# Dense pooled values: block-diagonal zeros taken out of an attention and gated-MLP kernel, and its order drawn up anew

## The chip, the cores and the metric

The kernel runs on one core of a Trainium2 chip. The metric is the device time of one execution in microseconds (us). TensorE is called PE, its weight loads PEld, VectorE DVE, ScalarE ACT, GpSimd POOL, and SyncE, which issues the DMAs here, SP.

## The reference

```python
B, H, S, D = 8, 8, 576, 64; factor = 4; Sd = S // factor; scale = 1 / sqrt(D)
q_d, k_d, v_d = (a.reshape(B, H, Sd, factor, D).mean(axis=3) for a in (q, k, v))
out_d = softmax(scale * q_d @ k_d.T) @ v_d            # pooled: 144 x 144
mask = abs(pos[:, None] - pos[None, :]) < factor      # local: 7 keys for a query
out_local = softmax(where(mask, scale * q @ k.T, -1e9)) @ v
attn = repeat(out_d, factor, axis=2) + out_local
x = attn.transpose(0, 2, 1, 3).reshape(B * S, H * D)  # 4608 x 512
out = (sigmoid(x @ w_gate) * (x @ w_val)) @ w_out     # 512 -> 1536 -> 512
```

All of it in fp32; q, k and w_gate are drawn some 6, 6 and 3 times larger than usual.

## The kernel before

**Units.** The attention is cut into 32 units, each two heads of one batch (unit u = 4 x batch + pair), with the two heads on the two halves of the 128 partitions. Units 0 to 7 (batches 0 and 1) are written in `early`, the other 24 in `later`. A unit's steps, by the names used below: loads `qk` (local q and k), `qkd` and `vd` (the same data with the four elements of a pool group side by side) and `vb` (v for the local part); `pb` sums q and k over the four, `vB` sums v; `s` makes the local scores, `sd` the pooled ones; both softmaxes go over DVE, ACT and POOL; `tt` and `dt` turn the weights; `od` is the pooled output and `x` the local one; `xa` adds them and `xh`, `xl` split the sum into two fp16 parts for the MLP.

**Block-diagonal operands.** `od` and the local `x` need a different v for each head. Before, v of the two heads stands in a 128x128 block-diagonal tile (`vdblk`, and `vtile` in `vflat`): the first head's 64 columns on the first 64 partitions, the second's on the others, zeros elsewhere, so that one product of 128x128 serves both. The zeros are set once at the start, and whoever fills a tile writes its two halves apart: `load_vb` with two DMAs, `vdb` and `vB` with two additions. `sd` and `s` multiply the heads apart, on 64 rows each.

**MLP.** 4608 tokens in nine chunks of 512. Weights come as 64-bit words, are put together by `pr` (ACT), `sh` and `jn` (DVE) and split into two fp16 parts (`hi` on ACT, `lo` on DVE). Chunk 0 makes 12 gate products `pg`, 12 value products `pv` and the output products `po`; it needs x of units 0 to 3 for its first `pg`. Chunk 1 does the same. Later chunks multiply pairs of blocks in seven products instead of eight (`bank`, `obank`), from sums of x that DVE and POOL prepare.

**The order.** All steps are entered as operations with an engine, a cost in us, what they follow, and the buffers they hold. A list scheduler in the kernel then places them, engine by engine, by due times (`GOALS`, `PACE`); its table of costs and goals sets the order in which each engine's instructions are written. Each engine runs its own instructions in that order and waits for the others by semaphores. Where the schedule leaves PE idle before the first `pg`, dummy products `awake` are put in.

Of the kernel before, what the change touches and what calls it, by code (L numbers as in the profile page):

```python
# [10 lines left out]
F32 = mybir.dt.float32  # L11
# [11 lines left out]
PACE = {'a0': -6.52, 'a': 6.04, 's0': 25.62, 'sp': 8.122, 'e': 2.9, 's': 0.15, 'sd': 0.65, 'tt': 13.18, 'dt': 13.95, 'do': 15.81, 'x': 16.17, 'b3': -0.21, 'b4': -2.69, 'b5': -3.01, 'b6': -1.13, 'b7': 3.85, 'extra': 0.41, 'ahead': 36}  # L23
GOALS = {'x0': 40.8, 'x0s': 7.26, 'pv': 72.16, 'pvs': 6.2, 'x1': 101.2, 'x1s': 19.48, 'po': 221.56, 'pos': 26.01, 'c1': 151.79}
INTURN = ("s", "sd", "tt0_", "tt1_", "dn", "dt", "vB", "do", "x0", "x1")
# [35 lines left out]
VTOF = (0, 1, 2, 3, 0, 1, 2, 0)  # L61
# [14 lines left out]
def attention_moe(ctx, tc, qk, qkd, v, vd, wg, wv, wo, mask, out):  # L76
# [68 lines left out]
    def zeroed(eng, shape, dtype, name):  # L145
# [4 lines left out]
    vdblk = [zeroed(nc.gpsimd, [P, NKC, P], F32, f"vdblk{i}") for i in range(2)]  # L150
    ad = zeroed(nc.gpsimd, [QM, 2, NKC, 2, WIN], F32, "ad")
    vblk = cp.tile([P, 2, NBLK, P], F16, tag="vblk", name="vblk")
    vring = cp.tile([P, NVR, NBLK * D], F32, tag="vring", name="vring")
    vflat = [x.rearrange("p (a b) -> p a b", a=NBLK) for x in (
        vring.rearrange("p a b -> p (a b)")[:, : NBLK * P], vring.rearrange("p a b -> p (a b)")[:, NBLK * P : 2 * NBLK * P],
        vblk.rearrange("p t b c -> p (t b c)").bitcast(F32), borrow(0, NBLK * P))]
    for i, t in enumerate(vflat):
        (nc.gpsimd if i % 2 else nc.vector).memset(t, 0.0)
    flat = {id(vblk): vblk.rearrange("p t b c -> p (t b c)").bitcast(F32)}
# [160 lines left out]
    def vload(u):  # L320
        vraw[u] = vring[:, NVR - 1 if u < NPLAIN else u % NVR].rearrange("p (a b) -> p a b", a=NBLK)
        nc.sync.dma_start(vraw[u], v[u])
# [124 lines left out]
    def zero(*tiles):  # L447

        for t in tiles:
            nc.gpsimd.memset(flat[id(t)], 0.0)  # L450
            own(t, "zero")
# [1351 lines left out]
```

## Time and profile before

| | |
|---|---|
| median of 3 runs | 989.0 us (986.9 to 991.27) |
| the profiled execution | 988.05 us, span 986.3 us |
| PE busy | 952.4 us, 97% of the span |
| DVE busy | 805.4 us, 82% |
| ACT busy | 656.9 us, 67% |
| POOL busy | 419.5 us, 43% |

The span reaches from the first to the last instruction. The busy time of PE holds its dummy products too, and the end of a matmul in the trace is modelled, so what a run of matmuls costs is read from its start to the start of the next operation.

### The profile page before, as it was taken

What the parts mean: (1) busy time and instruction counts of PE and PEld (TensorE: products, weight loads), DVE (VectorE), ACT (ScalarE), POOL (GpSimd) and SP (SyncE); (2) the same over time, 40 slices, a digit from 0 to 9 for tenths busy, and PEclk for the clock granted to TensorE, in tenths of its full rate; (3) what the DMA queues carried; (4) which work ended last, traced back from release to release, by engine and by line L of the source; (5) the groups of instructions that cost most, each with busy time, mean ns of one, the idle gap of its engine ahead of it and who ended that gap; (6) DMA issues with size and microseconds to landing.
All of it is one profiled execution on the core that took longest, in us unless ns stands there. A gap on an engine that the chain in (4) does not pass through costs nothing.

```text
span 986.3 us, 23787 instructions
## 1 busy us (share of the span) xinstructions
PE 952.4 (97%) x9412; PEld 738.1 (75%) x9412; DVE 805.4 (82%) x1430; ACT 656.9 (67%) x1650; POOL 419.5 (43%) x411
## 2 busy tenths in 40 slices
PE   7788999999999999989999999999999999999997
PEld 5654655455547677778888888888888988888885
DVE  6999998879999889889998888878788678556653
ACT  5888665656446776768777787777776865655551
POOL 4331323555456666445666565565543323000000
PEclk8999999999999999999999999999999999999999
DMA  9898888444435788677867766777555656666631
GB/s 313 287 316 274 295 300 262 161 169 153 178 137 197 255 278 251 191 264 273 285 237 259 269 234 249 231 283 269 200 203 193 231 179 217 214 220 209 230 128 44
DMA packets 78736, 225.36 MB, mean 228 GB/s; under 512 B 26656, under 2 KB 30240, under 8 KB 78368
## 3 DMA queue, kind: packets, MB, share of 16 engines
q1 hardware_dynamic: 78624, 223.83, 66.0%
q8 instruction: 74, 1.21, 0.5%
q14 instruction: 38, 0.31, 0.1%
HBM read 196.80 MB, written 27.00 MB: 227 GB/s over the span
## 4 chain that ended last, share of the span: by engine, by line
PE 78%; DVE 7%; issue 1%; ACT 1%; DVEq 0%
PE bank L868 35%; PE obank L1007 15%; PE po L431 10%; PE pg L431 4%; PE pv L431 4%; PE x L431 2%; PE s L436 2%; PE sd L436 2%; PE od L431 2%; PE at L555 1%; DVE wg L751 1%; DVE vblk L607 1%; PE adt L575 1%; DVE arena L748 1%; DVE wo L965 1%
## 5 line engine op out<-in xcount | busy, mean ns | idle before, releaser
L868 PE MATMUL bank<-arena,wv 128*128 128x256 f16 x1764 | 220.8, 273 | 5.4 <-DVE wg L898 4.0
L868 PE MATMUL bank<-arena,wg 128*128 128x256 f16 x1764 | 221.2, 273 | 0.1
L868 PEld LDWEIGHTS <-wv 128*128 128x128 f16 x1764 | 170.8, 98 | 31.5 <-issue 7.4
L868 PEld LDWEIGHTS <-wg 128*128 128x128 f16 x1764 | 171.4, 98 | 24.9 <-issue 1.0
L1007 PE MATMUL obank<-wo,spare 128*128 128x256 f16 x1071 | 147.3, 273 | 0.6 <-DVE wo L965 0.6
L1007 PEld LDWEIGHTS <-spare 128*128 128x128 f16 x1071 | 103.2, 98 | 13.9 <-issue 1.7
L965 DVE SCALAR_TENSOR_TENSOR wo<-wg,wo 128x512 f16<-128x512 f32 (+1 forms) x136 | 93.5, 705 | 19.8 <-ACT wo L962 19.5
L751 POOL TENSOR_TENSOR wg<-wg 128x256 f32<-128x256 f32 x50 | 40.9, 820 | 160.3 <-DVE wo L965 141.8
L962 ACT ACTIVATE wo<-wg 128x512 f16<-128x512 f32 (+1 forms) x136 | 76.4, 577 | 16.1 <-DVE wg L898 9.2
L431 PE MATMUL po<-spare,wo 128*128 128x512 f16 x324 | 79.4, 379 | 1.2 <-ACT arena L1138 1.2
L910 ACT COPY wv<-bank 128x512 f32<-128x512 f32 x84 | 49.1, 584 | 37.2 <-PE bank L868 36.3
L431 PEld LDWEIGHTS <-wo 128*128 128x128 f16 x432 | 40.8, 98 | 41.3 <-issue 2.8
L917 ACT COPY bank<-wv 128x256 f32<-128x256 f32 x84 | 31.7, 377 | 54.6 <-DVE wg L915 43.7
L431 PE MATMUL pv<-arena,wv 128*128 128x512 f16 x288 | 67.5, 384 | 0.1
L431 PE MATMUL pg<-arena,wg 128*128 128x512 f16 x288 | 67.4, 384 | 0.1
L915 DVE TENSOR_TENSOR wg<-bank,wv 128x512 f32<-128x512 f32 x63 | 43.4, 689 | 27.7 <-PE bank L868 25.9
L1007 PE MATMUL obank<-wo,wv 128*128 128x256 f16 x357 | 58.4, 273 | 0.0
L545 POOL TENSOR_TENSOR ad<-e,sme 72x288 f32<-72x288 f32 x48 | 37.6, 800 | 45.5 <-PE adt L575 27.7
L607 DVE SCALAR_TENSOR_TENSOR vblk<-vring,svb,vblk 64x640 f16<-64x640 f32 x48 | 54.7, 1139 | 0.6
L748 POOL TENSOR_TENSOR arena<-arena 128x512 f16<-128x512 f32 (+1 forms) x33 | 37.1, 1128 | 42.5 <-ACT arena L744 41.0
L517 POOL TENSOR_TENSOR t<-t,sm 128x768 f32<-128x768 f32 x24 | 38.1, 1586 | 33.5 <-DVE sm L523 22.7
L431 PEld LDWEIGHTS <-wg 128*128 128x128 f16 x288 | 27.8, 99 | 32.6 <-issue 2.3
(215 smaller groups left out, 2004.2 us busy)
## 6 DMA issues: line engine op xcount, KB each, us to landing
wg<-wg SPq DMA_DIRECT2D x42, 896.0 KB, 4.7
wv<-wv SPq DMA_DIRECT2D x42, 896.0 KB, 4.6
spare<-wo SPq DMA_DIRECT2D x51, 448.0 KB, 4.6
qk<-in_qk_dram SPq DMA_DIRECT2D x30, 610.0 KB, 4.8
qkd<-in_qkd_dram SPq DMA_DIRECT2D x29, 576.0 KB, 5.3
arena<-in_wo_dram SPq DMA_DIRECT2D x24, 512.0 KB, 5.3
vd<-in_vd_dram SPq DMA_DIRECT2D x29, 384.0 KB, 5.1
out_dram<-arena SPq DMA_DIRECT2D x16, 512.0 KB, 5.1
```

What stands on the lines that cost most here:

```text
L431: nc.tensor.matmul(o, w[a], x[c], start=first and i == 0, stop=last and i == len(pairs) - 1)
L436: nc.tensor.matmul(o, w, x, start=True, stop=True)
L517: engine(n("sb" if k == "mx" else "tm")).tensor_tensor(out=groups(), in0=groups(), in1=s[k].unsqueeze(2).to_broadcast([P, 4 * NH, WIN]), o ...
L607: nc.vector.scalar_tensor_tensor(out=VB[ps, 1, :, ps], in0=src, scalar=sc, in1=VB[ps, 0, :, ps], op0=ALU.mult, op1=ALU.subtract)
L748: eng.tensor_tensor(out=lo, in0=src, in1=hi, op=ALU.subtract)
L751: eng.tensor_tensor(out=o, in0=x, in1=y, op=ALU.subtract)
L868: nc.tensor.matmul(o, w[:, a, k], x[:, xb, k, c], start=start and z == 0, stop=z == len(mms) - 1, skip_group_check=True)
L910: op(f"sa_{n}_{i}", "A", 0.58, lambda i=i: nc.scalar.copy(snap(i)[:, HC:], banks[i]), [g(0), p("ad"), p("se")] + (["w1"] if n == 0 else []))
L915: lambda i=i: nc.vector.tensor_tensor(out=vsum(n) if i else duo(n)[:, 1], in0=banks[i], in1=snap(i)[:, :CH], op=ALU.add),
L962: nc.scalar.activation(g()[:, blocks, 0], src.rearrange("p (b t) -> p b t", t=HC), AF.Copy, scale=GSCALE)
L965: nc.vector.scalar_tensor_tensor(out=g()[:, blocks, 1], in0=src.rearrange("p (b t) -> p b t", t=HC), scalar=GSCALE, in1=g()[:, blocks, 0], ...
L1007: nc.tensor.matmul(obank[M][:, half], w[:, wb, a], g[:, xb, x], start=start and z == 0, stop=z == 5, skip_group_check=True)
```

## The change

It has four parts. First, the pooled v (`vdense`) and the v of the local part in units 0 to 7 are held dense, 64 columns for both heads; the products `od` and `x` are made by `heads`, one for each half: 64 rows by 64 columns, into that half's output partitions. The zeroing of the block-diagonal tiles falls away, `load_vb` is one DMA, `vB` one addition. Second, in batch 0 only q is summed in `pb`; the sum over k is made by PE, which accumulates four products whose moving operand steps over every fourth element, and the sum over v likewise, with the v factor as the stationary operand. Third, v of units 0 to 6 has seven buffers of its own instead of four. Fourth, the costs, goals and pace of the scheduler are new, and the order is made from them.

```diff
-GOALS = {'x0': 40.8, 'x0s': 7.26, 'pv': 72.16, 'pvs': 6.2, 'x1': 101.2, 'x1s': 19.48, 'po': 221.56, 'pos': 26.01, 'c1': 151.79}
+GOALS = {'x0': 50.0, 'x0s': 4.73, 'pv': 87.23, 'pvs': 5.86, 'x1': 94.08, 'x1s': 17.53, 'po': 220.49, 'pos': 30.55, 'c1': 162.23}
...
-VTOF = (0, 1, 2, 3, 0, 1, 2, 0)
+VTOF = (0, 1, 2, 3, 4, 5, 6, 0)
...
-    vdblk = [zeroed(nc.gpsimd, [P, NKC, P], F32, f"vdblk{i}") for i in range(2)]
+    vdense = [cp.tile([P, NKC, D], F32, tag=f"vdense{i}", name=f"vdense{i}") for i in range(2)]
...
-    for i, t in enumerate(vflat):
-        (nc.gpsimd if i % 2 else nc.vector).memset(t, 0.0)
...
     def load_vb(u):
         vtile[u] = vflat[VTOF[u]]
-        for ps in HALVES:
-            nc.sync.dma_start(vtile[u][ps, :, ps], v[u][ps])
+        nc.sync.dma_start(vtile[u], v[u])
...
+    def heads(o, w, x, first=True, last=True):
+
+        pairs = ((0, 0), (0, 1), (1, 0)) if len(w) == 2 else ((0, 0),)
+        for i, (a, c) in enumerate(pairs):
+            for ps in HALVES:
+                nc.tensor.matmul(o[ps], w[a][ps], x[c][ps], start=first and i == 0, stop=last and i == len(pairs) - 1)
...
         def vB():
             own(VDB, u)
-            for ps in HALVES:
-                nc.gpsimd.tensor_tensor(out=VDB[ps, :, ps], in0=y()[ps, :, 0], in1=y()[ps, :, 1], op=ALU.add)
+            nc.gpsimd.tensor_tensor(out=VDB.rearrange("p a b -> p (a b)"), in0=y()[:, :, 0], in1=y()[:, :, 1], op=ALU.add)
...
             for c in range(NKC):
-                product(pt[:, :SD], [VDB[:, c]], [s["adt"][:, c]], c == 0, c == NKC - 1)
+                heads(pt[:, :SD], [VDB[:, c]], [s["adt"][:, c]], c == 0, c == NKC - 1)
...
         def prep():
             x = qkdraw[u].rearrange("p (g f) -> p g f", f=4)
+            if first:
+                s["qd"] = wk.tile([P, 2, SD], F32, tag="qks", name=f"qks_{u}", bufs=1)[:, 0]
+                s["kd"] = [x[:, SD:, f] for f in range(4)]
+                x = x[:, :SD]
+                if chosen[n("pb")] == "V":
+                    nc.vector.tensor_reduce(s["qd"], x, axis=AX.X, op=ALU.add)
+                    return
...
         def pooled():
...
+            if first:
+                for qb in range(2):
+                    for f in range(4):
+                        for h, ps in enumerate(HALVES):
+                            nc.tensor.matmul(pts[h][:QM, qb * SD : (qb + 1) * SD], s["qd"][ps, qb * QM : (qb + 1) * QM], s["kd"][f][ps],
+                                             start=f == 0, stop=f == 3)
+                return
...
         def dout():
...
+            if first:
+                for c in range(NKC):
+                    for f in range(4):
+                        heads(pt[:, :SD], [vdraw[u][:, c, :, f]], [s["adt"][:, c]], c == f == 0, c == NKC - 1 and f == 3)
+                return
...
             for i in range(i0, i1):
-                product(pt[:, (i - i0) * R : (i - i0 + 1) * R], [vtile[u][:, i]], [s["at"][:, i]])
+                heads(pt[:, (i - i0) * R : (i - i0 + 1) * R], [vtile[u][:, i]], [s["at"][:, i]])
```

On SP, at the start of the program, the loads of units 0 to 3 stand like this before (`wo`, `wv` and `wg` are weight buffers that are borrowed for early units; the `in_v_dram` rows are `vb`, the `in_wg_dram` ones the MLP's weights):

```order
L399 DMA wo_116<-in_qkd_dram 128x1152
L407 DMA vd_184<-in_vd_dram 128x768
L407 DMA wv_115<-in_vd_dram 128x768 x3
L391 DMA qk_250<-in_qk_dram 128x1220
L414 DMA vring<-in_v_dram 64x10x64 x2
L399 DMA wo_116<-in_qkd_dram 128x1152
L391 DMA wo_116<-in_qk_dram 128x1220
L414 DMA vring<-in_v_dram 64x10x64 x2
L399 DMA wo_116<-in_qkd_dram 128x1152
L391 DMA wo_116<-in_qk_dram 128x1220
L414 DMA vblk<-in_v_dram 64x10x64 x2
L414 DMA wg_114<-in_v_dram 64x10x64 x2
```

The same stretch of SP with the change, up to the first two weight rows:

```order
L396 DMA wo_116<-in_qkd_dram 128x1152
L388 DMA qk_180<-in_qk_dram 128x1220
L404 DMA vd_233<-in_vd_dram 128x768
L404 DMA wv_115<-in_vd_dram 128x768 x3
L396 DMA wo_116<-in_qkd_dram 128x1152
L388 DMA wo_116<-in_qk_dram 128x1220
L396 DMA wo_116<-in_qkd_dram 128x1152
L410 DMA vring<-in_v_dram 128x640
L388 DMA wo_116<-in_qk_dram 128x1220
L410 DMA vring<-in_v_dram 128x640 x3
L223 DMA arena<-in_wg_dram 128x1024
L223 DMA arena<-in_wv_dram 128x1024 x2
```

Unit 1's q and k (`qk`) now stand ahead of the pooled v, units 2's and 3's pooled q and k ahead of the first v, and each v is one row of 128x640.

On PE, before the first `pg`, unit 2's turn of the pooled weights, of the local ones and its `od` stand like this before:

```order
L1282 MATMUL adt_616<-ident,ad 128x72 x6
L93 LDWEIGHTS idle
L93 MATMUL awake<-idle 128x256
L1237 MATMUL at_0_632<-ident,t_406 128x2x64 x3
L1237 MATMUL at_1_640<-ident,t_406 128x2x64 x3
L431 MATMUL od_654<-adt_2_617,vdblk_117 128x144 x3
```

And with the change, with unit 1's local output `x` among them:

```order
L1295 MATMUL adt_658<-ident,ad 128x72 x6
L448 MATMUL x_0_668<-at_1_515,vring 64x58 x16
L448 MATMUL x_1_688<-at_1_515,vring 64x58 x4
L1243 MATMUL at_0_695<-ident,t_382 128x2x64 x3
L448 MATMUL od_710<-adt_2_659,wv_115 64x144 x24
L1243 MATMUL at_1_744<-ident,t_382 128x2x64 x3
```

`od` has 24 products of half the height where it had three, and reads the raw v in `wv`; the dummies here are gone; `x` has 20 products of 64 rows where it had ten of 128.

On POOL, where the first units of `later` begin, the sums of v stand like this before (`vd` is the loaded v, `qkd` the loaded q and k, `ad` the pooled weights):

```order
L634 TENSOR_TENSOR qkd_1862<-qkd_1862 128x288x2
L1271 TENSOR_TENSOR ad<-e_1823,sme_1824 72x2x3x48 x2
L634 TENSOR_TENSOR vd_1830<-vd_1830 128x192x2
L585 TENSOR_TENSOR vdblk_117<-vd_1830 64x3x64 x2
L768 TENSOR_TENSOR arena<-wg_114 128x1024
L634 TENSOR_TENSOR vd_2051<-vd_2051 128x192x2
L585 TENSOR_TENSOR vdblk_119<-vd_2051 64x3x64 x2
```

With the change:

```order
L630 TENSOR_TENSOR vd_1572<-vd_1572 128x192x2
L630 TENSOR_TENSOR qkd_1693<-qkd_1693 128x288x2
L581 TENSOR_TENSOR vdense_117<-vd_1572 128x192
L1284 TENSOR_TENSOR ad<-e_1576,sme_1577 72x2x3x48 x2
L1492 MEMSET vblk 128x1280
L1359 TENSOR_TENSOR arena<-spare,arena 128x448
L1234 TENSOR_TENSOR t_1174<-t_1174,sm_1675 128x768
L630 TENSOR_TENSOR vd_1881<-vd_1881 128x192x2
L581 TENSOR_TENSOR vdense_118<-vd_1881 128x192
```

The second sum of v is one row of 128x192 where it was two of 64x3x64.

## Rows read from the trace of the kernel before

**Rows 1.** The page: the span, and of each engine the busy time, its share of the span and the instructions.

```profile
span 986.3 us, 23787 instructions
PE 952.4 (97%) x9412; PEld 738.1 (75%) x9412; DVE 805.4 (82%) x1430; ACT 656.9 (67%) x1650; POOL 419.5 (43%) x411
```

**Rows 2.** Busy time by stretch: the stretch, its length, busy time (and instructions) of each engine, the granted clock of PE as a share of full speed, the busy share of the DMA engines, GB/s.

```profile
0.00:55.38 55.38, 44.50 (x592) 36.02 (x592) 45.24 (x93) 39.20 (x121) 21.66 (x33) 0.94 0.91 301
55.38:148.40 93.02, 85.78 (x552) 46.42 (x547) 88.42 (x183) 68.96 (x164) 27.41 (x29) 0.96 0.87 294
148.40:987.00 838.60, 822.13 (x8277) 655.66 (x8275) 671.69 (x1155) 548.78 (x1367) 370.39 (x349) 1.00 0.63 216
...
10.00:30.00 20.00, 15.23 (x198) 12.32 (x198) 13.69 (x32) 14.23 (x48) 9.83 (x14) 0.83 0.97 280
30.00:55.38 25.38, 20.77 (x307) 17.61 (x305) 24.60 (x52) 21.31 (x65) 7.52 (x9) 1.00 0.90 323
...
100.00:125.00 25.00, 24.53 (x190) 14.27 (x189) 24.10 (x47) 15.43 (x40) 9.57 (x9) 1.00 0.88 286
...
300.00:600.00 300.00, 289.70 (x3233) 239.42 (x3232) 264.84 (x449) 219.67 (x584) 177.96 (x167) 0.99 0.74 254
```

**Rows 3.** The same view of the dummy products `awake` alone: stretch, length, PE busy (and instructions), clock, DMA.

```profile
0.00:55.38 55.38, 13.27 (x81) 0.94 0.91 301
```

**Rows 4.** PE's instructions in order of time before the first `pg`: start, length, line, operation, output<-input, shape (rows*columns of the weights, then output), count; in brackets the idle time before and what ended it. An fp32 product counts as two.

```profile
7.22 0.71 PE L436 MATMUL sd<-qks 64*72 64x144 f32 x8
...
18.61 1.56 PE L1212 MATMUL s<-qk 64*64 64x64 f32 x48 [1.99 <-DMA qk<-in_qk_dram]
...
27.60 0.71 PE L436 MATMUL sd<-qks 64*72 64x144 f32 x8
28.24 0.60 PE L1282 MATMUL adt<-ident,ad 72*128 72x72 f32 x6
...
39.35 0.90 PE L431 MATMUL od<-adt,vdblk 128*128 128x144 f32 x6
40.09 0.60 PE L93 MATMUL awake<-idle 128*128 128x256 bf16 x4
...
50.82 2.44 PE L431 MATMUL x<-at,wg 128*128 128x58 f32 x20
53.10 1.36 PE L93 MATMUL awake<-idle 128*128 128x256 bf16 x11
...
54.58 0.87 PE L1212 MATMUL s<-qk 64*64 64x64 f32 x48
55.38 0.82 PE L431 MATMUL pg<-arena,wg 128*128 128x512 f16 x3
```

**Rows 5.** SP's queue in order of time: start and length of the issuing of DMAs.

```profile
13.17 1.36 SPq L391 DMA_DIRECT2D wo<-in_qk_dram x1
14.63 3.89 SPq L414 DMA_DIRECT2D vring<-in_v_dram x2
18.56 0.97 SPq L399 DMA_DIRECT2D wo<-in_qkd_dram x1
19.57 0.43 SPq L391 DMA_DIRECT2D wo<-in_qk_dram x1
20.10 3.92 SPq L414 DMA_DIRECT2D vblk<-in_v_dram x2
24.11 4.05 SPq L414 DMA_DIRECT2D wg<-in_v_dram x2
28.21 1.40 SPq L226 DMA_DIRECT2D arena<-in_wg_dram x1
```

**Rows 6.** The DMA view of 10 to 32 us in 40 slices of 0.55 us: busy share of the DMA engines in tenths, GB/s, and the packets with their sizes.

```profile
DMA  9999999999999999999999999999997311490969
GB/s 385 413 408 391 432 443 412 345 279 278 188 251 250 278 398 414 355 269 271 183 236 298 260 360 401 400 290 238 177 237 178 91 28 37 98 223 18 145 259 432
DMA packets 6534, 6.08 MB, mean 276 GB/s; under 512 B 5384, under 2 KB 5384, under 8 KB 6531
```

**Rows 7.** DVE's first instructions in order of time, columns as in rows 4.

```profile
1.21 1.12 DVE L158 MEMSET vring<- 128x1280 f32 x1 [0.22 <-issue]
2.56 1.12 DVE L158 MEMSET vblk<- 128x1280 f32 x1 [0.22 <-issue]
...
5.82 1.35 DVE L1197 TENSOR_REDUCE qks<-qkd 128x288 f32<-128x1152 f32 x1 [0.69 <-DMA qkd<-in_qkd_dram]
7.09 0.41 DVE L237 TENSOR_SCALAR wg<-wg 128x512 int32<-128x512 int32 x1
7.54 0.69 DVE L241 SCALAR_TENSOR_TENSOR wg<-arena,wg 128x512 int32<-128x512 int32 x1
```

**Rows 8.** The instructions on the tile `vdblk`, by engine: count, least/median/longest ns, first and last start in us, shapes; and POOL's sums of v by line, with their busy time and mean ns.

```profile
L585 POOL TENSOR_TENSOR vdblk<-vd x48: 525/612/1394, 157.6 to 741.0; 64x192 f32<-64x192 f32 x48
...
L1292 DVE TENSOR_REDUCE vdblk<-wv x2: 935/942/949, 30.6 to 31.6; 64x192 f32<-64x768 f32 x2
...
L585 POOL TENSOR_TENSOR vdblk<-vd 64x192 f32<-64x192 f32 x48 | 35.1, 730 | 9.8 <-PE od L431 7.3
```

**Rows 9.** All engines in order of time around 424 us, columns as in rows 4.

```profile
422.42 2.30 POOL L545 TENSOR_TENSOR ad<-e,sme 72x288 f32<-72x288 f32 x1 [2.56 <-PE adt L575]
...
423.78 0.41 DVE L816 TENSOR_TENSOR arena<-spare 128x256 f32<-128x256 f32 x1
...
424.23 2.83 DVE L816 TENSOR_TENSOR arena<-arena,spare 128x256 f32<-128x256 f32 x1
...
429.33 2.11 PE L868 MATMUL bank<-arena,wv 128*128 128x256 f16 x12 [2.34 <-DVE wg L898]
```

More of the change, by code (lines that the diff above doesn't have):

```diff
@@ L1290, in vdb @@
             if chosen[n("vB")] == "V":
-                for ps in HALVES:
-                    nc.vector.tensor_reduce(VDB[ps, :, ps], vdraw[u][ps], axis=AX.X, op=ALU.add)
+                nc.vector.tensor_reduce(VDB, vdraw[u], axis=AX.X, op=ALU.add)
                 return
             nc.gpsimd.tensor_tensor(out=x[:, :, 0:2], in0=x[:, :, 0:2], in1=x[:, :, 2:4], op=ALU.add)
-            for ps in HALVES:
-                nc.gpsimd.tensor_tensor(out=VDB[ps, :, ps], in0=x[ps, :, 0], in1=x[ps, :, 1], op=ALU.add)
+            nc.gpsimd.tensor_tensor(out=VDB.rearrange("p a b -> p (a b)"), in0=x[:, :, 0], in1=x[:, :, 1], op=ALU.add)
         def dout():
@@ L1356, in early @@
         unit_op("vd", "D", 1.3, lambda: load_vd(u), new=[] if ring else [("vd", "vd_")])
-        unit_op("vb", "D", 1.7, lambda: load_vb(u), new=[(f"vt{VTOF[u]}", "v_")])
-        unit_op("pb", "V", 1.27, prep, ["qkd"], new=[("qks", "qks_")], use=["qkd_"], alt=("P", 2.1))
+        unit_op("vb", "D", 1.3, lambda: load_vb(u), new=[(f"vt{VTOF[u]}", "v_")])
+        unit_op("pb", "V", 0.68 if first else 1.27, prep, ["qkd"], new=[("qks", "qks_")], use=["qkd_"], alt=("P", 1.2 if first else 2.1))
         unit_op("s", "E", 1.3, scores, ["qk", "mq!"], new=[("bank", "s0_"), ("bank", "s1_"), ("t", "t_")], use=["qk_"])
@@ L1372, in early @@
                     use=[f"a{par}_", "at_"])
-        unit_op("sd", "E", 0.75, pooled, ["pb"], new=[("bank", "d0_"), ("bank", "d1_"), ("e", "e_")], use=["qks_"])
+        unit_op("sd", "E", 1.7 if first else 0.75, pooled, ["pb"], new=[("bank", "d0_"), ("bank", "d1_"), ("e", "e_")], use=["qks_", "qkd_"] if first else ["qks_"])
         for h in range(2):
             unit_op(f"dm{h}_", "V", 0.44, lambda h=h: dtop(h), ["sd"], use=[f"d{h}_"])
-            unit_op(f"de{h}_", "A", 1.35, lambda h=h: dexp(h), [f"dm{h}_"] + ["de0_"] * h,
+            unit_op(f"de{h}_", "A", 1.2, lambda h=h: dexp(h), [f"dm{h}_"] + ["de0_"] * h,
                     use=[f"d{h}_", "e_"])
@@ L1379, in early @@
         unit_op("rd", "V", 0.16, lambda: recip("sme"), ["sec"])
-        unit_op("dn", "A" if first else "P", 1.62 if first else 1.5, dnorm, ["rd"], new=[("ad", "ad_")], use=["e_"])
+        unit_op("dn", "A" if first else "P", 1.4 if first else 1.5, dnorm, ["rd"], new=[("ad", "ad_")], use=["e_"])
         unit_op("dt", "E", 0.5, dturn, ["dn"], new=[("bank", "ta_"), ("adt", "adt_")], use=["ad_"])
         unit_op("dc", "A", 0.53, dturned, ["dt"], use=["ta_", "adt_"])
-        unit_op("vB", "V", 1.75, vdb, ["vd", "vm"], new=[(f"vdb{u % 2}", "vdb_")], use=["vd_"], alt=("P", 2.35))
-        unit_op("do", "E", 0.8, dout, ["dc", "vB"], new=[("bank", "do_"), ("od", "od_")], use=["adt_", "vdb_"])
+        if first:
+            unit_op("do", "E", 1.7, dout, ["dc", "vd"], new=[("bank", "do_"), ("od", "od_")], use=["adt_", "vd_"])
+        else:
+            unit_op("vB", "V", 0.95, vdb, ["vd", "vm"], new=[(f"vdb{u % 2}", "vdb_")], use=["vd_"], alt=("P", 1.6))
+            unit_op("do", "E", 0.6, dout, ["dc", "vB"], new=[("bank", "do_"), ("od", "od_")], use=["adt_", "vdb_"])
         unit_op("oc", "A", 0.43, dcopy, ["do"] + ["vs0!"] * first, use=["do_", "od_"])
@@ L1472, in attention_moe, with zero @@
     op("arena", "N", 0.0, lambda: None, ["st1", "st3", "pv11"] + [f"loo{i}_" for i in range(NFC)])
-    op("zero", "P", 3.3, lambda: zero(vblk), ["x16"])
+    def zero():
+        nc.gpsimd.memset(vblk32, 0.0)
+        own(vblk, "zero")
+    op("zero", "P", 1.3, zero, ["x15", "x16"])
     op("head", "A", 0.62, lambda: nc.scalar.copy(xf(2)[:, :, : 2 * WIN], head), ["arena"] + [f"xl{u}" for u in range(NPAIR, NPLAIN)])
@@ L1543, in all_turns @@
         return sorted(t, key=lambda k: t[k])
[L1546 removed]
+    CAPS = dict(qk=2, qkd=1, vd=1, vt0=1, vt1=1, vt2=1, vt3=1, vt4=1, vt5=1, vt6=1, qks=1, t=3, at=2, e=1, ad=1, adt=1, vdb0=1, vdb1=1, od=2, xs=1, stage=NST, wa=2,
                 tanh=2, g16=3, att=2, gate=1, val=1, o0=1, o1=1, o2=1, o3=1)
```

64 lines of the change are left out of this document (30 added, 34 removed).

## The prediction

> **What bounds the kernel now.** I read the page first, for the totals: PE is busy 952 of 986 us, DVE 805 [rows 1]. Busy shares hide stages, so next the busy times in three stretches cut at PE's first gate product (55.38 us) and at its first output product (148.40 us) [rows 2]. After 148.40 PE is busy 822.1 of 838.6: there PE is the bound, and the reader sees 10.3 of its 16.5 idle us between 300 and 600. Between the cuts DVE is busy 88.4 of 93.0 and PE 85.8: DVE leads, until PE catches up (24.5 of 25 us busy from 100 on). Before 55.38 nothing is full: DVE has 45.2, and of PE's 44.5 us 13.3 are `awake`, dummy products [rows 3]. So the third place to look is the start. PE's timeline shows the scores of unit 1 waiting 1.99 us for the load of its q and k [rows 4]. SP's own timeline says why the load is late: the two half-loads of a v tile hold the queue for about 3.9 to 4.1 us, three times, and the first weights after the opening one are issued at 28.21 [rows 5]. In the DMA view of 10 to 32 us, 5384 of 6534 packets are under 512 B, the rate falls from 385-443 to below 250 GB/s, and at 27 to 29 us the queues run nearly dry [rows 6]. DVE is idle 6.3 of the 20 us from 10 to 30 and 0.8 of the 25 after that [rows 2]. The start is paced by loads until about 30 us and by DVE from there.
>
> **The change, part by part.**
>
> *v loaded whole.* Eight units' v arrives in one piece of 128x640 instead of two of 64x10x64, and the queue is reordered so that unit 1's q and k go ahead of the pooled v. The DMA view moved 6.08 MB in 22 us at a mean of 276 GB/s; at the 400 GB/s of its own slices with big packets the same bytes take 15.2, so loads at the end of this stretch can be up to 6.8 us earlier [rows 6].
>
> *PE work in batch 0.* The pooled scores `sd` took 0.64 us from their first product to the next operation (27.60 to 28.24) and now have four times the products in equal pairs: 2.56, +1.92. The pooled output `od` took 0.74 (39.35 to 40.09); three products become 24 half-size ones, twelve pairs: 2.96 if a pair costs what one whole product did, +2.22. The local output `x` took 2.28 (50.82 to 53.10); its 10 products become 10 pairs of 64x64 products. The nearest row is that of the scores, whose 48 matmuls of 64x64 run four at a time, 12 rounds in 0.80 us (54.58 to 55.38), 0.067 a round; 20 rounds are 1.33, -0.95. If pairs do not run side by side it is 2.67, +0.39 [rows 4]. Per unit +3.19, four units +12.8, and all of it lies where PE now runs dummies.
>
> *DVE and POOL before the first gate product.* DVE loses two memsets of 1.12, two q/k sums of 1.35 for three of half the size (an estimate: 0.7 each), and one block-diagonal v sum of 2 x 0.94 [rows 7, 8]. That is 2.2 + 0.6 + 1.9; but the memsets end before the first pooled load lands and DVE waits 0.69 for that load [rows 7], so they give nothing: 2.5 counts.
>
> *When the first gate product starts.* Two bounds. PE: real work so far 44.5 - 13.3 = 31.2, plus 12.8 is 44.0; from the first `sd` at 7.22 that ends at 51.2 if PE never waits. DVE: 45.2 - 2.5 - 2.2 of work and 10.1 + 2.2 of idle make 52.9, and if earlier loads halve its 6.3 idle us, 49.7. I take 51.5, 3.9 earlier, between 49.7 and 55.4 (no gain, if the longer `sd` and `od` eat it). DVE does not carry all of that onward: by the order it has by then joined two weight tiles fewer (two shifts and joins, 2 x (0.41 + 0.69) = 2.2) [rows 7], and has more of unit 4's softmax done. I take 1.3 of it as owed, so the lead that the DVE-bound stage starts with is **-2.6** (0 to -4.4).
>
> *x of units 4 to 7.* -0.95 each on PE. Unit 4's falls into the DVE-bound part, the other three where PE is full: **-2.9** (-3.8 to +1.6).
>
> *od of units 4 to 31.* Three whole products become six halves. If pairs run side by side, as row-split `sd` and four-way `s` do [rows 4], **0**; if not, +0.74 x 24 = +17.8 in the PE-bound part alone. I take 0: a quarter-array round of 0.067 us for four is hard to explain with products in single file. What the scores do not show is two products from different row halves going to one PSUM bank, as the new pairs do; their two row halves go to two banks.
> The Trainium skill, "TensorEngine Tiling (Array Packing)", Restrictions and Gotchas, says of exactly this that different row tiles cannot access the same PSUM bank at the same time. By that rule the pairs would go in single file and the sum would be some 25 us worse (the second rival); no row here shows it either way.
>
> *Strided operands in batch 0.* The k and v factors are now read by PE at every fourth element. No row has a strided operand; the lower bound is nothing, the upper is that `sd` and `od` take twice as long, (2.56 + 2.96) x 4 = 22 us more before the first gate product. I take nothing, since a 4-byte PE pass here already moves half a column per cycle (0.120 us for 144 columns at 2.4 GHz, from 0.74 / 6), and keep the upper end as a rival.
> The Trainium skill, "SBUF — State Buffer", Door 1, says that accesses which each cross into a new 16-byte line pay a penalty; a step of four fp32 is exactly one line. By it the strided passes are slower, and with the upper end as their price the run would come to 995.7 (the third rival); no row here shows it.
>
> *v sums of later units.* POOL's two half-size additions per unit (48, mean 730 ns, 35.1 us) become one [rows 8]: some 17.5 us off POOL. POOL has room. But DVE pays beside it: one 128x256 subtraction took 2.83 where its twin just before took 0.41, while POOL ran a 2.30 us operation, and PE then waited 2.34 us for DVE [rows 9]. The order also hands six of DVE's subtractions on x (L751) to POOL. Of the 10.3 idle PE us between 300 and 600 I take off **-1.5** (0 to -6). The whole later order is shuffled as well, which may put DVE's long passes elsewhere: +8 at worst, about today's idle time again.
>
> **Sum.** -2.6 - 2.9 + 0 - 1.5 = -7.0: span 979.3. The profiled execution took 988.05 for a span of 986.3, so 1.75 lies outside: 981.05. Its own time is 0.95 below the median 989.0, so **982.0**.
>
> **Rivals.**
> *The start gains nothing.* The longer `sd` and `od` sit in each unit's chain (+4.1 a unit), and if chains, not loads, set DVE's idle time, the first product stays at 55.4. For it: DVE's idle gaps before 30 us are waits on PE as well as on loads. Against: PE has 13 us of dummies. -2.9 - 1.5 remain at most, or -2.0 with half of them: 984.5 to 988. Chance 0.20.
> *Pairs in single file* (slower than before). Mechanism: both halves of `od` and `x` write one bank and PE runs them one after the other. +17.8 later, 4 x (2.96 + 1.33) = 17.2 more before the first gate product, which then starts at 68.4, 13.0 later, less the 7.2 idle us that PE has in the next stage, and +1.6 for `x` of units 4 to 7: 986.3 + 25.2, as a run 1014. It decides from about 0.3 us per later `od` on, where 24 of them eat the 7.0. Chance 0.07.
> *Strided reads at half speed* (slower). +22 on PE: first gate product at 73, 17.7 later; the next stage has 7.2 idle us to give back and `x` 3.8: +6.7, 995.7. If only `sd` pays, 10.2, the give-back covers it. Chance 0.05.
> *The new order stalls PE elsewhere* by up to 8: 983 to 991. Chance 0.10, half of it slower than 0.5%.
> *More than forecast*: start at 49.7 (-4.4), `x` in full (-3.8), half the later idle gone (-6): 974.8. Chance 0.13.
> *The forecast*, 978 to 986: 0.45, most of it below 984.
>
> **Chances.** 0.5% (4.9 us) is about what a measurement of this kernel can tell from no change. Faster: 0.13 + 0.42 = 0.55. Same: 0.20 + 0.03 + 0.05 = 0.28. Slower: 0.07 + 0.05 + 0.05 = 0.17. The range 973 to 994 leaves out the single-file case, most of the strided one and the far end of the gain.
>
> **What would show it.** Right: unit 1's scores start at about 12 us, not 18.61, and no v load holds SP for 3 us; the first gate product near 51.5 with some 10 dummies' less time; `od` of later units at 0.74 and `x` of 58 f32 columns at about 1.3; DVE full from 30 to 100. Wrong: a later `od` above 1 us (single file), `sd` of batch 0 above 3 us (strided), the first gate product at 55 or later, or PE idle over 18 us after the first output product.

## The result and the profile after

The changed kernel took 1002.8 us (median of four runs, 1002.6 to 1003.7), the kernel before beside it 988.1: 1.013 times as long, with a 95% interval of 1.011 to 1.016 (the two medians alone give 1.015). The forecast was 982.0, its range 973 to 994: the change is slower, and by more than the range allows.

The page of the changed kernel, lines as in [rows 1]:

```profile
span 1000.5 us, 24849 instructions
PE 971.6 (97%) x9971; PEld 739.3 (74%) x9971; DVE 804.0 (80%) x1420; ACT 659.4 (66%) x1650; POOL 397.9 (40%) x375
```

PE, busy for 97% of the span as before, is busy 19.2 us longer, and 24 without the dummies (48 of them now, 8.1 us, where 81 took 13.3 [rows 3]). The same three stretches as in [rows 2], cut at the first gate product and at the first output product of this kernel (columns as there):

```profile
0.00:60.20 60.20, 56.34 (x903) 43.75 (x903) 36.55 (x87) 38.06 (x125) 11.85 (x19) 1.00 0.74 279
60.20:166.52 106.32, 94.15 (x740) 49.18 (x736) 100.04 (x191) 74.55 (x175) 33.73 (x34) 0.90 0.82 285
166.52:1000.00 833.48, 821.14 (x8335) 646.36 (x8333) 667.41 (x1144) 546.77 (x1353) 352.33 (x324) 1.00 0.62 214
```

All that is lost is lost ahead of the first output product: it comes at 166.5 us in place of 148.4, 18.1 later (4.8 in the first stretch, 13.3 in the second). Behind it the new kernel is 3.9 us quicker. The start has changed hands: PE is busy 56.3 of 60.2 us, and DVE, busy 45.2 of 55.4 before, only 36.6 of 60.2. PE's timeline says with what (columns as in [rows 4]):

```profile
12.71 0.89 PE L1218 MATMUL s<-qk 64*64 64x64 f32 x48
...
22.93 3.22 PE L448 MATMUL od<-adt,vd 64*64 64x144 f32 x48
26.08 4.30 PE L1258 MATMUL sd<-wo,qks 64*72 64x144 f32 x32
30.31 0.55 PE L1243 MATMUL at<-ident,t 128*128 128x128 f32 x3
...
42.81 1.38 PE L448 MATMUL x<-at,vring 64*64 64x58 f32 x40
44.12 0.55 PE L1243 MATMUL at<-ident,t 128*128 128x128 f32 x3
```

From start to start, `od` of batch 0 takes 3.15 us, `x` 1.31, and `sd` 4.23, where it was forecast at 2.56. What that does to DVE is in its waits up to 62 us (what waited, for whom, us in all, times, longest):

```profile
DVE mxd L1265 <- PE sd L1258: 7.9, 3, 3.3
DVE qks L1194 <- PE sd L1258: 4.4, 1, 4.4
```

DVE stands still for 12.3 us because a pooled score is not ready or its input not yet free; before, the first of these waits was 0.2 us and the second not there. In the next stretch PE pays: of its 12.2 idle us (7.2 before) most are waits for DVE.

```profile
PE mxt L266 <- DVE hmx L194: 3.9, 1, 3.9
PE mxt L266 <- DVE vm L334: 2.7, 1, 2.7
PE pg L427 <- DVE wg L260: 2.4, 2, 1.9
PE od L448 <- DVE spare L1343: 1.8, 1, 1.8
```

Before, the waits of that stretch were spread over POOL, DVE, a load and ACT:

```profile
PE at L1237 <- POOL t L1228: 2.0, 1, 2.0
PE adt L1282 <- DVE t L1221: 1.7, 1, 1.7
PE s L1212 <- DMA qk<-in_qk_dram: 1.5, 1, 1.5
PE at L1237 <- ACT at L1240: 1.0, 1, 1.0
```

The granted clock of the stretch (the mean, as a share of full speed) is lower too, 0.90 where it was 0.96, so part of the 8.4 us that PE is busy longer there can be clock and not work: in e13 below, the same products at 0.98 keep it busy 6.7 us less. Whether the lower clock adds to the delay or only follows from PE's waits, no run here tells.

### The profile page after: what moved, and what is told of

The parts are those of the page before. It is cut to its first block, busy times and chain, and to the rows that moved or that the text cites. A ratio compares the mean times of both kernels' runs of the same rounds, so it can differ in the third digit from the quotient of the medians.

```text
span 1000.5 us, 24849 instructions
## 1 busy us (share of the span) xinstructions
PE 971.6 (97%) x9971; PEld 739.3 (74%) x9971; DVE 804.0 (80%) x1420; ACT 659.4 (66%) x1650; POOL 397.9 (40%) x375
## 4 chain that ended last, share of the span: by engine, by line
PE 78%; DVE 17%; issue 3%; ACT 1%; DMA 0%; DVEq 0%; SPq 0%; ACTq 0%
PE bank L864 36%; PE obank L1003 16%; PE po L427 6%; PE pv L427 3%; PE od L448 3%; PE pg L427 3%; PE x L427 2%; PE s L432 2%; PE sd L432 1%; PE sd L1258 1%; PE at L552 1%; DVE wo L260 1%; DVE spare L1106 1%; DVE vblk L603 1%; DVE arena L812 1%
## 5 line engine op out<-in xcount | busy, mean ns | idle before, releaser
L864 PEld LDWEIGHTS <-wv 128*128 128x128 f16 x1764 | 170.3, 98 | 28.6 <-issue 4.7
L747 POOL TENSOR_TENSOR wg<-wg 128x256 f32<-128x256 f32 x62 | 50.6, 818 | 175.6 <-DVE wo L961 130.1
L961 DVE SCALAR_TENSOR_TENSOR wo<-wg,wo 128x512 f16<-128x512 f32 (+1 forms) x136 | 95.9, 726 | 19.8 <-ACT wo L958 19.5
L427 PE MATMUL pg<-arena,wg 128*128 128x512 f16 x288 | 70.1, 393 | 2.4 <-DVE wg L260 2.4
L427 PEld LDWEIGHTS <-wo 128*128 128x128 f16 x432 | 40.1, 98 | 43.1 <-issue 2.6
L744 POOL TENSOR_TENSOR arena<-arena 128x512 f16<-128x512 f32 (+1 forms) x33 | 40.0, 1217 | 57.7 <-ACT arena L740 57.7
L427 PEld LDWEIGHTS <-wv 128*128 128x128 f16 x288 | 28.3, 100 | 34.6 <-issue 4.0
```

Of the source, the lines that this page charges most:

```text
L427: nc.tensor.matmul(o, w[a], x[c], start=first and i == 0, stop=last and i == len(pairs) - 1)
L744: eng.tensor_tensor(out=lo, in0=src, in1=hi, op=ALU.subtract)
L747: eng.tensor_tensor(out=o, in0=x, in1=y, op=ALU.subtract)
L864: nc.tensor.matmul(o, w[:, a, k], x[:, xb, k, c], start=start and z == 0, stop=z == len(mms) - 1, skip_group_check=True)
L961: nc.vector.scalar_tensor_tensor(out=g()[:, blocks, 1], in0=src.rearrange("p (b t) -> p b t", t=HC), scalar=GSCALE, in1=g()[:, blocks, 0], ...
```

## The experiments

Two theories. T1: PE's accumulated sums, above all the strided k, make PE the bound of the start, DVE waits there, and what DVE did not get done delays the next stretch. T2: the new order as such puts the weight work late. All runs are in one table. A ratio is to executions of the kernel before that were made beside that run, whose median lies between 988.1 and 990.4; where two rows are compared, the ratios say more than the medians. The last three columns are of the one profiled execution, which lies above the median by 4.7 us in e11, 2.6 in e17, 2.5 in e6 and 1.4 in e9, and below it by 2.2 in e7 and 1.8 in e5. e3, e6 and e8 do not give the reference's result: they show what an order costs in time, and are no versions to use.

| kernel | us, median | ratio to before (95%) | first gate product | first output product | behind it |
|---|---|---|---|---|---|
| before | 988.1 | | 55.4 | 148.4 | 837.9 |
| the change | 1002.8 | 1.0132 (1.0106 to 1.0159) | 60.2 | 166.5 | 834.0 |
| e1 k in blocks | 996.6 | 1.0067 (1.0052 to 1.0083) | 55.8 | 161.0 | 833.8 |
| e17 k every second | 997.0 | 1.0071 (1.0052 to 1.0089) | 57.1 | 163.6 | 833.8 |
| e2 k summed on DVE, POOL | 995.7 | 1.0060 (1.0041 to 1.0079) | 54.8 | 159.5 | 833.9 |
| e5 and v to a quarter | 993.6 | 1.0049 (1.0031 to 1.0068) | 51.9 | 155.6 | 834.1 |
| e4 true costs | 997.5 | 1.0079 (1.0059 to 1.0099) | 64.3 | 164.2 | 831.4 |
| e3 old goals | 1010.2 | 1.0203 (1.0186 to 1.0219) | 59.5 | 167.4 | 841.1 |
| e8 k in blocks, true costs | 1026.4 | 1.0382 (1.0357 to 1.0407) | 59.2 | 160.7 | 864.1 |
| e7 dense only, new plan | 987.9 | 0.9989 (0.9974 to 1.0004) | 55.2 | 152.3 | 831.6 |
| e6 dense only, old plan | 995.2 | 1.0064 (1.0041 to 1.0087) | 52.5 | 150.0 | 845.9 |
| e9 e7, `od` four times | 994.6 | 1.0048 (1.0028 to 1.0068) | 61.6 | 162.9 | 831.3 |
| e10 e9, `sd` six times | 996.9 | 1.0079 (1.0055 to 1.0104) | 63.8 | 163.1 | 831.3 |
| e11 e7, mixed goals | 987.0 | 0.9987 (0.9962 to 1.0012) | 51.1 | 153.8 | 835.7 |
| e12 e11, old costs | 996.0 | 1.0065 (1.0041 to 1.0089) | 51.3 | 159.8 | 835.8 |
| e13 the change, half joins | 997.5 | 1.0071 (1.0050 to 1.0092) | 60.8 | 160.1 | 835.6 |
| e14 before, half joins | 989.3 | 0.9982 (0.9956 to 1.0007) | 54.9 | 150.4 | 838.8 |
| e15 e7, maxima on ACT | 991.0 | 1.0011 (0.9988 to 1.0033) | 53.4 | 149.8 | 837.3 |
| e16 e11, maxima on ACT | 985.7 | 0.9961 (0.9943 to 0.9979) | 54.0 | 145.8 | 838.0 |

### The stride of the moving operand

In e1, e17, e2 and e5 every engine's instructions stand in the order of the change. In e1 the elements that one product reads lie side by side; in e17 they are two apart.

```diff
# e1
-                s["kd"] = [x[:, SD:, f] for f in range(4)]
+                kf = qkdraw[u][:, S:].rearrange("p (f g) -> p f g", f=4)
+                s["kd"] = [kf[:, f] for f in range(4)]
# e17
+                kf = qkdraw[u][:, S:].rearrange("p (a g f) -> p a g f", a=2, f=2)
+                s["kd"] = [kf[:, f // 2, :, f % 2] for f in range(4)]
```

> The changed kernel, in which batch 0's k is laid out in memory in four blocks of 144, so that the moving operand of each pooled score product has its elements side by side; the order on every engine is that of the change, instruction for instruction. Theory T1 (the operand with a stride of four elements is what I priced wrongly, and TensorE binds the start): the 32 instructions of one unit's pooled scores fall from 4.23 us to 2.1 to 2.6 us, the first gate product from 60.2 us to 52.5 to 55, and the time from 1002.8 us by 5 to 8 to 995 to 998. Theory T2 (the new order binds: VectorE's weight joins stand late, so that the weight loads and the stage after wait for them): the pooled scores fall as much, the first gate product comes a few us earlier at most, and the stage behind it gives that back: 1000 to 1003.

> The change with batch 0's k laid out so that the moving operand of the pooled scores takes every second element (in the change every fourth, 4.30 us for the 32 instructions of a unit; side by side 2.18). If the price grows with the distance, 2.7 to 3.6 us for a unit and 998 to 1000 us; if any distance but one element costs the same, 4.2 to 4.4 and 1002 to 1003; if two neighbours come in one read, 2.1 to 2.3 and 996 to 997.5.

The third unit's `sd` in PE's timeline, of e1 and then of e17:

```profile
25.87 2.18 PE L1259 MATMUL sd<-wo,qks 64*72 64x144 f32 x32
```

```profile
27.08 2.26 PE L1259 MATMUL sd<-wo,qks 64*72 64x144 f32 x32
```

A step of four fp32 elements costs 4.30 us, a step of two 2.26, and side by side it is 2.18. So a step of two costs next to nothing, and a step of four doubles the time. Most of the price reaches the end: 4 x 2.12 = 8.5 us less of PE's work brings the first gate product 4.4, the first output product 5.5 and the end 6.2 us forward (6.4 by the ratios). T1 holds for this part, and it is a good 40% of the loss.

### The rest of the k sum, and the v sum

e2 puts the whole k sum back on DVE and POOL; e5 also takes only one of the four positions of v, so that PE has no more to do than before the change.

```diff
# e2: the two branches "if first" of prep and pooled are taken out
# e5, beside that
-                    for f in range(4):
-                        heads(pt[:, :SD], [vdraw[u][:, c, :, f]], [s["adt"][:, c]], c == f == 0, c == NKC - 1 and f == 3)
+                    heads(pt[:, :SD], [vdraw[u][:, c, :, 0]], [s["adt"][:, c]], c == 0, c == NKC - 1)
```

> The changed kernel with the sums of pooled k in batch 0 made by VectorE and GpSimd again, as before; the pooled scores of a unit are 4 products in place of 16, and every other instruction stands where the change puts it. T1: TensorE loses 4 x (4.23 - 0.64) = 14 us of work in the start, VectorE gains some 4 x 0.6; the first gate product comes at 47 to 52 us, and the time is 988 to 993. T2: the stage after the start waits for VectorE as in the changed kernel, with its joins where they were, and the time stays at 997 to 1002.

> The kernel in which VectorE and GpSimd sum batch 0's k again, and beside that the pooled outputs of batch 0 take only one of the four positions of v (12 products in place of 48; three quarters of the sum are left out). The order is that of the change on every engine. TensorE so does no more in the start than before the change. T1 (the accumulated v sums on TensorE are the rest of the loss): 4 x (3.15 - 0.8) = 9 us leave TensorE, the first gate product comes at 46 to 50 us in place of 54.8, and the time is 986 to 990. T2 (where the new order puts the weight joins is the rest of the loss): the first gate product stays at 53 to 55 and the first output product within 2 us of 159.5, and the time is 993 to 996.

e2 lies between what the two theories said. It is 0.9 us below e1, less than the intervals can tell: side by side, the k sum on PE costs about what it saves. e5 gains 2.1 by the medians (the ratios, 1.0060 and 1.0049, differ by less than either interval), in its profiled execution 3.8, not 9: a little for T1, more for T2. It still has its first output product 7.2 us later than the kernel before, with the added work of PE gone (busy 129.7 us up to there, dummies included, and 130.3 before).

### The dense values alone, and PE's added work in their order

e7 has all of the change but batch 0's sums on PE, with the change's goals, paces and costs; e6 the same with the old ones.

> The dense values alone (dense pooled v, dense first v with one load each in seven places, products by heads), with batch 0's sums on VectorE and GpSimd as before and the scheduler's goals, paces and costs of the kernel before. My prediction's terms for this part: x of units 4 to 7 -2.9, the rest of GpSimd and its port -1.5, the earlier loads at most -2.2: 981 to 987, beside 990.4 for the kernel before. T1 and T2 both give that. If it is 989 or more, the terms of the dense part were wrong as well.

> The dense values alone as in the run beside it, under the goals, paces and costs of the change. T1 (the accumulated sums are the loss, the plan is not): within 3 us of the run beside it, 980 to 988. T2 (the plan is the loss): 8 to 12 us over the run beside it, 992 to 998, with the joins as late as in the change and the first output product at 157 us or later.

e7 comes out level with the kernel before: its first output product 4.0 us later, and 6.3 us less behind it. Batch 0's sums, with the order that goes with them, are the whole loss. e6 missed what both theories said: the old tables do not suit the new operations, and lose 8 us behind the first output product. e7 missed both as well: it is 7 us under e6, where T1 had the two within 3 us and T2 had e7 8 to 12 over. e9 and e10 keep e7's order and only add work on PE, by repeating products whose last set counts:

```diff
# e9 and e10, in dout                       # e10 also, in pooled
+            for again in range(4 if first else 1):
                 for c in range(NKC):
                     heads(pt[:, :SD], [VDB[:, c]], [s["adt"][:, c]], c == 0, c == NKC - 1)
...
+            for again in range(6 if first else 1):
                 each(pooled_pairs(s, pts))
```

> The dense values alone under the plan of the change (987.9 us), with the pooled output products of batch 0 made four times over (48 in place of 12 for a unit, each set starting anew, so the last counts): TensorE has the change's v work, VectorE and GpSimd keep their sums, and the order is that of the kernel with dense values alone. T1 (TensorE's added work in the start makes VectorE wait there): 4 x 2.3 = 9 us more TensorE work, VectorE's idle time up to the first output product grows from 19.5 by 4 to 9 us, time 992 to 997. T2 (the order found with the sums in is the loss, TensorE's work is covered): the idle time grows by less than 2 us, 987 to 990.

> As the run beside it, and the pooled scores of batch 0 made six times over besides (6 x 0.64 = 3.84 us for a unit; the change takes 4.23 with the strided operand). TensorE then has nearly all of the work that the change gives it in the start, and the order is still that of the dense values alone. T1: VectorE waits for the pooled scores as in the change (12.3 us there for two kinds of instruction), and the time is 998 to 1004. T2: 988 to 992.

The first two stretches of e7, then of e9 (columns as above):

```profile
0.00:55.15 55.15, 44.05 (x710) 33.11 (x711) 42.39 (x95) 42.56 (x136) 24.04 (x33) 0.94 0.87 325
55.15:152.34 97.19, 86.02 (x721) 45.34 (x719) 90.42 (x183) 69.71 (x174) 36.11 (x34) 0.96 0.84 295
```

```profile
0.00:61.62 61.62, 51.63 (x854) 42.49 (x855) 43.27 (x94) 43.19 (x138) 24.50 (x34) 0.92 0.79 295
61.62:162.86 101.25, 89.01 (x719) 45.45 (x718) 92.20 (x185) 70.33 (x173) 33.04 (x33) 0.93 0.82 284
```

The added `od` work alone moves the first gate product by 6.5 us and the time by 6.6 (5.8 by the ratios), with DVE's work up to the first output product the same within 3 us and its idle time there up from 19.5 to 27.4. The dummies did not make room: 11.5 us of them still run in e9's first 66 us, 13.0 in e7's, and the first gate product is late all the same. PE is in the chain of each unit, and what it does longer, DVE waits for longer. T1 holds here. The repeated `sd` of e10 adds only 2.4 us: 996.9, under the 998 to 1004 of T1, and DVE waits 4.5 us for `sd`, not 12.3. Its first stretch:

```profile
0.00:63.76 63.76, 57.32 (x1014) 49.06 (x1015) 42.94 (x96) 43.50 (x138) 23.76 (x33) 0.99 0.78 284
```

The 160 further instructions would take 10.9 us at e1's 68 ns each, but PE's busy time grows by 5.7 and its idle time falls from 10.0 to 6.4: the granted clock is 0.99 there, 0.92 in e9, so PE's work ran quicker, and part of the added work found a gap.

### Orders

e3 gives the changed kernel the old goals and paces; e4 gives the scheduler the measured costs of the two sums; e8 is e1 with such costs; e11 and e12 are dense values alone with the old goals for the start and the new paces behind.

```diff
# e3: PACE and GOALS of the kernel before
# e4
-        unit_op("sd", "E", 1.7 if first else 0.75, ...
+        unit_op("sd", "E", 4.3 if first else 0.75, ...
-            unit_op("do", "E", 1.7, dout, ["dc", "vd"], ...
+            unit_op("do", "E", 3.15, dout, ["dc", "vd"], ...
# e11: 'x0', 'x0s', 'pv', 'pvs', 'x1', 'x1s' of GOALS from the kernel before; e12: its costs and INTURN as well
```

> The changed kernel's operations and costs with the scheduler's table of goals and paces of the kernel before: the order alone differs. T1: TensorE still carries the same 37 us of accumulated sums in the start, the first gate product is at 58 to 63 us, and the time 998 to 1006. T2: the joins come earlier, SyncE's weight loads are held for less than 10 us, and the time is 985 to 993.

> The changed kernel with the scheduler's own costs of the two accumulated sums in batch 0 set to what the trace showed (4.3 us for the pooled scores in place of 1.7, 3.15 for the pooled outputs in place of 1.7): operations unchanged, the order alone differs (three of the six first weight joins stand some 15 instructions earlier on VectorE). T1: TensorE's work in the start is the same, the first gate product at 57 to 62 us, the time 996 to 1004. T2: an order that knows of TensorE's load brings VectorE's weight work forward, and the stage after the start waits less: 985 to 995.

> The change with batch 0's k laid out in blocks (contiguous moving operand) and the scheduler's costs of the accumulated sums at what the traces showed (2.2 us for the pooled scores, 3.15 for the pooled outputs). If the two gains measured apart (-6.2 for the blocks, -5.3 for the costs) act on different work, they add up: 990 to 993. If both only shorten the same wait, 994 to 997.

> The dense values alone with the goals of the kernel before for the first two batches and the stage up to the first output products, and the change's goals and paces for the rest. The dense part gained 6.3 us behind the first output product and lost 4.0 ahead of it (152.3 us in place of 148.4). T1: what was lost ahead is a matter of the order there, so that the first output product comes at 148 to 151 us and the time is 981 to 985, under both kernels. If the dense part itself costs the start something, the first output product stays at 152 or later and the time at 987 to 990.

> As the run beside it, with the scheduler's costs of the kernel before in place of the change's. The run with the dense values under all of the old tables had its first output product at 150.0 us but took 846 us behind it; with the change's paces behind it should take 831 to 835: 981 to 986. If the time behind the first output product stays over 840, it is the costs and not the paces that make that part slow.

The order is worth as much as the operations. e3, at 1010.2, is slower than the change and outside what either theory said: its first output product comes 0.9 us later still, and 7.1 us more lie behind it. True costs alone take 5.3 us off the change, though the first gate product comes 4.1 us later: by it DVE has 43.1 us of work done, not 36.6. The two gains did not add: e8 loses 30 us behind the first output product, where PE is idle 25 us between 300 and 600, at these waits among others:

```profile
PE od L448 <- DVE at L565: 5.4, 3, 3.1
PE s L432 <- ACT e L536: 3.8, 2, 2.5
PE mxt L173 <- DVE at L565: 3.3, 1, 3.3
```

e11 brings the first gate product at 51.1, where the forecast had it, and gains nothing: its next stretch is 102.7 us long (in a profiled execution 4.7 us above the median). e12, forecast at 981 to 986, loses ahead of the first output product (159.8) and not behind it (835.8), so behind it the paces and late goals made e6 slow, and not the costs. e7 and e12 have the same operations and lie 8 us apart.

### Does DVE bound the way to the first output product?

e13 and e14 leave out half of the columns of the weight joins, in the change and in the kernel before, each in its own order.

```diff
-        nc.vector.scalar_tensor_tensor(out=a, in0=wtile[k, i, n][:, :, 0], scalar=29, in1=a, ...
+        a, b = a[:, : WPC if k == "o" else WPC // 2], wtile[k, i, n][:, : WPC if k == "o" else WPC // 2, 0]
+        nc.vector.scalar_tensor_tensor(out=a, in0=b, scalar=29, in1=a, ...
```

> The change with the joins of the gate and value weights on VectorE done on the first half of each tile's columns only (128x256 in place of 128x512; the low words of the other half are left out): 24 x 0.73 x 1/2 = some 8 us less of VectorE's work ahead of the first output product, all else in the order of the change. If VectorE bounds the way to the first output product (its work there 136.6 us plus the 29.9 us in which it idles), that product comes 6 to 9 us earlier, at 158 to 161, and the time is 994 to 997. If TensorE's start or the transfers bound it, 1001 to 1003.

> The kernel before with the same half of the joins left out. If VectorE bounds the way to the first output product there as well (133.7 us of work plus 14.7 of idling in 148.4), it comes 6 to 9 us earlier and the time is 980 to 983; if TensorE or the transfers do, 987 to 990.

The second stretch of e13, then of e14:

```profile
60.84:160.11 99.27, 87.48 (x740) 46.06 (x736) 93.58 (x191) 74.36 (x175) 32.49 (x34) 0.98 0.88 306
```

```profile
54.89:150.44 95.55, 86.84 (x551) 46.51 (x546) 86.26 (x183) 68.02 (x163) 25.46 (x30) 0.95 0.82 285
```

In the change, the edit takes 7.5 us off DVE's work up to the first output product (136.6 to 129.1) and brings that product 6.4 us and the end 5.3 us forward. That is what the theory of a stretch bound by DVE forecast, and DVE is busy 94% of that stretch with and without the edit. But the granted clock there also rose, from 0.90 to 0.98, and PE was busy 6.7 us less with the same products; this run does not set the two apart.

In the kernel before, the time is the one expected if PE or the transfers bound the stretch (989.3, in 987 to 990). It is a weak test, though: there the same edit takes only 2.4 us off DVE's work (133.7 to 131.3), since other DVE operations took longer. PE is busy 19.7 to 19.9 of each 20 us from 95 to 135 there, and DVE 18.6 to 19.1. That the two engines were level before, and that the change tipped the stretch to DVE, fits these rows and is not shown by e14.

### A version that takes work off DVE

e15 and e16 find the magnitude of the value weights on ACT, as for the gate weights, in the plans of e7 and e11.

```diff
-        if k == "g":
+        if k in "gv":
...
-            op(f"ab{key}", *(("A", 0.64) if k == "g" else ("V", 0.68)), lambda k=k, i=i: wmax(k, i), [f"jn{key}"])
+            op(f"ab{key}", *("A", 0.64), lambda k=k, i=i: wmax(k, i), [f"jn{key}"])
```

> The dense values alone under the change's tables (987.9), and the magnitude of each value and output weight tile found by ScalarE, as that of the gate weights is, in place of VectorE's 24 reductions of 0.67 us: 16 us of work go from VectorE, which has 19.5 us of idling in the 152.3 us to the first output product, to ScalarE, which is busy there for 112. If VectorE bounds that stretch, the first output product comes 8 to 14 us earlier and the time is 974 to 981, faster than both kernels; if a new order loses it again, 984 to 990.

> The same with the goals of the kernel before for the start (987.0 without the move). By the same reckoning 973 to 980, or 983 to 990 if the order loses it.

The edit reached only the value weights (12 reductions, 8 us), not the output ones as the expectation says. e16 has its first output product at 145.8 and is the one version faster than both kernels, by 0.4%; the stretch behind it is 838.0 us. So its time falls in the second of the ranges expected: its first output product comes 8.0 us ahead of e11's (whose profiled execution lies 4.7 us above its median), and at the end 1.3 are left by the medians. e15, at 991.0, misses both ranges: 2.5 us gained ahead of that product, 5.7 lost behind it.

## Why the prediction was wrong

**Loads: right.** Unit 1's scores run from 12.71 us (12 forecast), no v load holds SP, and from 10 to 32 us 9.08 MB move at 413 GB/s with 300 packets under 512 B, against [rows 6].

```profile
DMA packets 2719, 9.08 MB, mean 413 GB/s; under 512 B 300, under 2 KB 300, under 8 KB 2716
```

**`x`, `od` and the pairs: right in the mechanism.** `x` 1.31 us (1.33), `od` of batch 0 3.15 (2.96). A later `od` was put at no change. From its start to the next operation, its three pairs of halves take 0.88 us (the median of units 8 to 31), where the three whole products took 0.74 [rows 4]: 24 x 0.14 = 3.4 us on PE that the sum lacks.

```profile
126.60 0.95 PE L448 MATMUL od<-adt,vdense 64*64 64x144 f32 x12
127.48 2.88 PE L427 MATMUL pg<-arena,wg 128*128 128x512 f16 x12
```

The single-file rival, which would have doubled these times, falls: the products of the two row halves write one PSUM bank here and run side by side, at a small price. The Trainium skill, "TensorEngine Tiling (Array Packing)", Restrictions and Gotchas, says that different row tiles cannot access the same PSUM bank at the same time; as a statement on time, the runs do not bear it out here.

**Strided operands: the step that failed.** It said "I take nothing". `od`, whose strided operand is the stationary one, did pay next to nothing (3.09 to 3.15 us a unit, and 3.04 to 3.09 in e9 with as many products and no stride, but for its first unit, which ran while the granted clock was down), but `sd` took 4.23 in place of 2.56: 4 x 1.67 = 6.7 us more on PE than forecast. e1, which takes the whole 8.5 us of the stride away, shows 6.2 us at the end. The rival for it stood at 0.05 with the sentence "If only `sd` pays, 10.2, the give-back covers it": the price was bounded rightly, the cover was wrong. The Trainium skill, "SBUF — State Buffer", Door 1, wants two accesses to each 16-byte line for full speed; a step of two fp32 elements makes two, a step of four one. The runs agree with that: 2.26 us, and 4.30. The same paragraph counts four fp32 elements as the step that is still free; for TensorE's moving operand the measurement says that two is nearly free and four is not (three was not run).

**The cover by dummies and the give-back: the second failed step.** The forecast laid all of the added work "where PE now runs dummies", and a late start into the idle time of the next stretch. It gave DVE at most 12.3 us of idle time ahead of the first gate product ("10.1 + 2.2 of idle"); it had 23.7, 12.3 of them waiting for `sd`. PE's bound of 51.2 "if PE never waits" came with 48.2 us of real work (56.34 - 8.11) in place of 44.0, and waits. The rivals counted the 7.2 idle us of PE in the next stretch as room for a late start. Of these only 2.1 were waits for DVE (2.0 were for POOL, 1.5 for a load, 1.3 for ACT), so reading whom they wait for would not have given the failure away. With DVE owing work they became 12.2, nearly all for DVE: the joins there rose from 18 to 20 as reckoned, but DVE's work as a whole from 88.4 to 100.0 us. e9 shows the first half of this, that more PE work in the start lengthens DVE's idle time. The second half, that in the changed kernel the first output product then waits for DVE, rests on PE's waits and on e13, where the clock changed as well.

**SP.** The early weights did come early, and then their buffers were not freed: DVE had joined only two tiles of each kind by 60.2 us, and SP waited from 27.5 to 47.1 for one of them.

```profile
SPq L223 <- DVE wg L238: 19.6, 1, 19.6
```

**Later terms: right in sign.** The stretch behind the first output product is 3.9 us shorter, where POOL's relief was to give 1.5 (the x of units 4 to 7, forecast at 2.9, now all lie ahead of it; three of them did before). POOL's sums of v are one operation a unit in place of two [rows 8], and PE is idle some 13 us there in place of some 16 [rows 2]. But tables alone move this stretch by more (845.9 us in e6, 831.6 in e7), so what gave the 3.9 is not shown.

**What stays open** is how much the change's order costs by itself. Taking PE's v work out of that order gives 2.1 us (e5), putting it into e7's order costs 6.6 (e9), and e5 is 5.7 slower than e7 without the work in dispute; e5 lacks DVE's v sums as well, so the last number is no clean price of the order. e10, with nearly the change's work on PE but e7's order, is 5.9 us under the change, and true costs take 5.3 off it; both point to the order, and neither holds all else the same. By the ratios, in us of 988: dense values -1.1, the v sum and the order that goes with it +7.0 (e7 to e2), the k sum side by side +0.7, its stride +6.4, in sum the 13.0 of the change. The steps add up by construction, and each has an interval of some 2 us or more.

One figure of the prediction is off by itself: in its first rival, half of 2.9 + 1.5 is 2.2, not 2.0, and would put the upper end at 987, not 988. Nothing hangs on it.

## What to carry to other kernels

Work moved to the engine that is full over the kernel as a whole has to be priced with its operand's layout, and dummies beside it are no room if the product stands in a chain that another engine waits for. Before counting on a later stretch to give a delay back, ask what work the delay leaves undone on the other engines: here PE's waits in the next stretch were mixed before, and nearly all for DVE once DVE had been kept waiting in the start. And an order can cost as much as the operation it was found for: run the operations and the order apart.

## What the runs showed of the hardware

An `sd` instruction whose moving fp32 operand is read at every fourth element takes 134 ns (4.30 us for 32) where it takes 68 side by side and 71 at every second (2.18 and 2.26). The same step in the stationary operand lengthens the weight load, from 133 to 190 ns by the median, and not the products (282/283 ns either way), behind which the load is hidden: 48 instructions take 3.15 us with the step and 3.07 without it (e9's third unit). A pair of half products on the two row halves, into one PSUM bank, costs a little more than one whole product: three pairs 0.88 us, three whole ones 0.74. In the changed kernel, instructions on the tile `od` (ns, least, median and longest):

```profile
L448 PEld LDWEIGHTS od<-adt,vdense x336: 129/133/133, 70.8 to 791.5; 64*64 64x64 f32 x168
L448 PEld LDWEIGHTS od<-adt,wv x144: 188/190/213, 34.9 to 54.7; 64*64 64x64 f32 x144
L448 PE MATMUL od<-adt,wv x144: 282/283/394, 35.0 to 54.8; 64*64 64x144 f32 x144
```
